# Hashed attention and a Fourier mixing block on one core: seven sorted pairs, sixteen classes, transfers in written order

## The chip, the core and the metric

The kernel runs on one core of a Trainium2 chip. The core has a matrix engine (TensorE, PE in the profile, with its weight loads as PEld), a vector engine (VectorE, DVE), a scalar engine (ScalarE, ACT), GpSimd (POOL) and SyncE (SP). SP's only work here is to issue DMA transfers; POOL issues the transfers whose rows are picked by an index (indirect DMA). The metric is the device time of one execution in microseconds (us), the median of several runs.

## What is computed

Two stages follow each other, both in float32. The first is attention in which a query sees only the keys that fall into the same hash bucket:

```
q, k, v: (4, 8, 768, 64);  proj: (64, 6)
q_bits = einsum('bhsd,dk->bhsk', q, proj) > 0      # six bits per token
q_bucket = sum(q_bits * 2**arange(6))              # 0..63; k_bucket alike
mask = q_bucket[..., :, None] == k_bucket[..., None, :]
attn = softmax(where(mask, q @ k.T / 8, -1e9))
attn_out = attn @ v
```

The second takes x, the attention's output as (4, 768, 512):

```
mixed = real(fft(fft(x, axis=1), axis=2));  u = x + mixed
un = (u - mean(u)) / sqrt(var(u) + 1e-6)
out = u + relu(un @ w_ch1) @ w_ch2                 # 512 -> 2048 -> 512
```

## The kernel before

The work goes by batch b (4) and by pair of heads n (16 in all, four per batch; a pair fills the 128 partitions with two heads of 64). `attention(b)` runs the four pairs of a batch in 24 steps, six per pair, one for each chunk of 128 keys; it yields after each step. `mix(b)` is the second stage of a batch: two folds by symmetry, a Fourier transform along the channels (tile `cs`, table `ch`, L1471) and along the sequence (tiles `A` and `B`, table `sq`, L1500), and then the two products with the weights in a seven-product scheme (`h_p`, L1777, and `o`, L1652). The main loop interleaves `attention(b)` with `mix(b - 1)`; the last `mix` runs alone. Batch 0's attention stands beside the arrival of the weights, under a manual schedule in which PE, DVE, ACT and POOL keep the written order. After it a planner orders each engine's instructions by its own estimate of times, apart from edges given by hand: `issue_after` and `behind` queue an instruction after a given one on its engine.

An **ordinary** pair computes all 768 x 768 scores: `weigh` (L1201) makes scores (L1223), exponentials (L1227) and the bucket mask (L1233), sums go into `acc` (L1359), `values` multiplies with v (L1244). Six pairs, 8, 9, 10, 12, 13 and 14 (`SORT`), are **sorted**: queries and keys are brought into the order of their buckets, so that a chunk of 128 keys needs only a window of the queries. `weigh_sorted` (L1094: scores L1106, exponentials L1110, mask L1118, sums L1125 and L1126) and `values_sorted` (L1131) work on windows of 224 or 320 columns (`SLACK` = 96 on each side). Sorting a pair has these parts:

- `rank(n)` (L880) loads q and k (L583), transposes them (L890), takes their squares for a norm (L763), computes the bits (`ubits`, L894, L900) and the bucket number of each token (`ids`, `bid`). Then, for the keys and again for the queries, it compares the numbers with 0 to 63 (`one`, L938), adds up over the six chunks (L946), counts with a matmul (`cnt`, L951), makes first and last places with a scan (L956, L959), adds it all up in PSUM (`rk`, L965 to L971), and picks each token's row (L986, L990, L996). The rows of the keys are ready some steps before those of the queries. A gap check (L977, L980) writes to `strange`: if any entry of it is positive, a flag (L1924) makes a general kernel, `_any_scores`, run after this one.
- Copies of k and v (`kvn`, and the slot of pair 3 in the last batch's x) and of q (`qnat`) are loaded on SP (L919, L927). Twelve indirect transfers on POOL scatter k and v to DRAM (`kvd`), twelve scatter q (`qsd`, all L1002).
- `fetch_sorted` (L1020) reads them back on SP in sorted order (L1023), at the first step of the pair before; `prepare_sorted` (L1051) transposes them (L1058) at the second.
- After the pair, `unsort` (L1155) transposes the result (L1159), writes it to DRAM (`osd`, L1164), gathers the rows back with twelve indirect transfers (L1172), and turns them with PE (`back`, L1182).

`ranks` (L1288) is called in every step from batch 1 on; it advances the running ranks by one part each, and starts one when its step comes (`START`, L1286): pairs 8, 9 and 10 at steps 0, 8 and 15 of batch 1, pair 12 at step 22 of it, 13 and 14 at steps 8 and 15 of batch 2.

The table `ch` is no constant tile: `mix` loads it into a part of `tq` (L1449 to L1452), whose other use is to hold temporaries of the product `o` (L1671 to L1706). The left factors of `h_p` are fetched from DRAM into a ring of 12 (w<-ad, L1745), the right factors of `o` in sets of seven (w<-bd, L1657), all on SP. `rs` (L1536, on POOL) is the row scale that the additions after `o` need.

Of the kernel before, what the change touches and what calls it, by code (L numbers as in the profile page):

```python
# [11 lines left out]
F32 = mybir.dt.float32  # L12
# [38 lines left out]
SLACK = 96  # L51


def _consts():
# [54 lines left out]
    so = np.zeros((P, 3 * P + D + 8))  # L109
# [3 lines left out]
    so[:, 3 * P : 3 * P + D] = np.arange(D)  # L113
    for r in range(P):
        h, bit = divmod(r % 32, NBITS)
        if h < 2:
            so[r, 3 * P + D + r // 32 * 2 + h] = 2.0**bit
# [382 lines left out]
def _main(  # L500
# [54 lines left out]
    SORT = (8, 9, 10, 12, 13, 14)  # L555

    def load(n, names="qkv", second=nc.sync):
# [6 lines left out]
        for nm in names:  # L564
# [14 lines left out]
            for i in range(4):  # L579
                s = src[b, 2 * t + i // 2, :, i % 2 * 32 : i % 2 * 32 + 32]  # L580
                d = tl[32 * i : 32 * i + 32]
                if nm == "k" or n in SORT:
                    nc.sync.dma_start(  # L583
                        d.rearrange("p (j a) -> p j a", a=32),
                        s.rearrange("(j b) a -> b j a", b=32),
                    )
                else:
                    s = s.rearrange("(j b r) a -> r b j a", b=32, r=2)
                    d = d.rearrange("p (r j a) -> r p j a", r=2, a=32)
                    for r in range(2):  # L590
                        nc.sync.dma_start(d[r], s[r])
# [34 lines left out]
    for i in range(NPK):  # L626
        pk = const.tile([P, 2, 2, HALF + 1], F32, tag=f"pk{i}", name=f"pk{i}")
        nc.gpsimd.memset(pk[:, :, :, HALF : HALF + 1], EPS)
        pks.append(pk)
    mean = const.tile([P, P], F32, tag="mean", name="mean")  # L630
# [241 lines left out]
    win = []  # L872
    for c in range(NT):
        win.append((max(0, c * P - SLACK), min(S, (c + 1) * P + SLACK)))
# [3 lines left out]
    eye, iota, pw8 = mb[:, 0:P].bitcast(F16), mb[:, P : P + D], mb[:, P + D : P + D + 8]  # L878

    def rank(n):  # L880

        b, t = divmod(n, NPAIR)
        load(n, "qk")
        yield
        r1 = wt([P, 3 * HALF], F32, "rank", f"rank{n}", 1)
        ut = r1[:, 0:S]
        bits = pt([P, HALF], f"ubits{n}")
        for io, nm in enumerate("qk"):
            tn = nat.pop((nm, n))
            nc.vector.transpose(ut, tn)  # L890
            norm(n, io, tn)
            for g in range(2):
                j = 2 * io + g
                nc.tensor.matmul(  # L894
                    bits[32 * j : 32 * j + 32, :], pj, ut[:, g * HALF : (g + 1) * HALF],
                    start=True, stop=True,
                )
            yield
        bt = wt([P, HALF], BF16, "bt", f"ubt{n}", 1)
        nc.vector.tensor_scalar(bt, bits, 0.0, None, op0=ALU.is_gt)  # L900
        ps = pt([P, 3, 8], f"ids{n}")
        for i in range(3):
            nc.tensor.matmul(
                ps[:, i, :], bt[:, i * P : (i + 1) * P], pw8, start=True, stop=True
            )
        bid = wt([P, 2, NT, 2], BF16, "bid", f"bid{n}")
        for io in range(2):
# [4 lines left out]
        kvn = [  # L912
            wt([P, 3, 2, 2, D], F32, "kvn", f"kvn{n}", 1),
            xs[b - 1][:, NPAIR - 1].rearrange("p (c h i d) -> p c h i d", c=3, h=2, i=2),
        ]
        for g in range(2):
            for i, src in enumerate((k, v)):
                for h in range(2):
                    nc.sync.dma_start(  # L919
                        kvn[g][:, :, h, i, :],  # L920
# [3 lines left out]
                    )  # L924
        qn = wt([P, NT, 2, D], F32, "qnat", f"qnat{n}", 1)
        for h in range(2):
            nc.sync.dma_start(  # L927
                qn[:, :, h, :], q[b, 2 * t + h].rearrange("(c p) d -> p c d", p=P)
            )
        yield  # L930
        one = r1[:, 0:HALF].bitcast(BF16).rearrange("p (c x) -> p c x", c=NT)
        upto = r1[:, HALF : 2 * HALF].bitcast(BF16).rearrange("p (c x) -> p c x", c=NT)
        kept = upto.bitcast(F16)
        m = r1[:, 2 * HALF : 3 * HALF]
        small = m.bitcast(BF16)
        total, ends = small[:, 0:P], m.bitcast(F16)
        for io in (1, 0):
            nc.vector.tensor_tensor(  # L938
                one.rearrange("p c (h x) -> p (c h) x", h=2),
                bid[:, io].rearrange("p c h -> p (c h)")[:, :, None].broadcast_to(  # L940
                    [P, 2 * NT, D]
                ),
                iota[:, None, :].broadcast_to([P, 2 * NT, D]), op=ALU.is_equal,
            )
            for c in range(2, NT + 1):
                nc.vector.tensor_tensor(  # L946
                    upto[:, c] if c < NT else total,
                    one[:, 0] if c == 2 else upto[:, c - 1], one[:, c - 1], op=ALU.add,
                )
            cnt = pt([P, P], f"cnt{io}_{n}")  # L950
            nc.tensor.matmul(cnt, onesb, total, start=True, stop=True)  # L951
            if io:
                last_, first_ = kept[:, 1], kept[:, 0]
            else:
                last_, first_ = ends[:, P : 2 * P], ends[:, 2 * P : 3 * P]
            nc.vector.tensor_tensor_scan(  # L956
                last_, onesb, cnt, 0.0, op0=ALU.mult, op1=ALU.add
            )
            nc.vector.tensor_tensor(first_, last_, cnt, op=ALU.subtract)  # L959
            yield  # L960
            ps = ps_sc.tile([P, 2, 512], F32, tag="sc", name=f"rk{io}_{n}")
            for g in range(2):
                o = ps[:, g, 0:HALF].rearrange("p (c x) -> p c x", c=3)
                cs = slice(3 * g, 3 * g + 3)
                nc.tensor.matmul(o, tri, one[:, cs], start=True, stop=False)  # L965
                if g == 0:
                    nc.tensor.matmul(o[:, 1], onesb, one[:, 0], start=False, stop=False)
                    nc.tensor.matmul(o[:, 2], onesb, upto[:, 2], start=False, stop=False)
                else:
                    nc.tensor.matmul(o, onesb, upto[:, cs], start=False, stop=False)  # L970
                nc.tensor.matmul(  # L971
                    o, eye, first_[:, None, :].broadcast_to([P, 3, P]), start=False, stop=True
                )
            if io == 0:
                gap = ends[:, 3 * P : 5 * P].rearrange("p (i x) -> p i x", i=2)
                for i, (e, f) in enumerate(((kept[:, 1], first_), (last_, kept[:, 0]))):
                    nc.vector.scalar_tensor_tensor(  # L977
                        gap[:, i], e, -float(SLACK + 1), f, op0=ALU.add, op1=ALU.subtract
                    )
                nc.vector.tensor_reduce(  # L980
                    strange[:, NW + n : NW + n + 1], gap, axis=AX.XY, op=ALU.max
                )
            rk = wt([P, NT, 2], F32, "rk", f"rk{io}_{n}", 1)
            for g in range(2):
                cs = slice(3 * g, 3 * g + 3)
                nc.vector.tensor_tensor(  # L986
                    m.rearrange("p (c x) -> p c x", c=3), one[:, cs],
                    ps[:, g, 0:HALF].rearrange("p (c x) -> p c x", c=3), op=ALU.mult,
                )
                nc.vector.tensor_reduce(  # L990
                    rk[:, cs].rearrange("p c h -> p (c h)"),
                    m.rearrange("p (c x) -> p c x", x=D), axis=AX.X, op=ALU.add,
                )
            tag, bufs = ("rowk", 1) if io else ("rowq", 7)
            rows[io, n] = wt([P, NT, 2], I32, tag, f"row{io}_{n}", bufs)
            nc.vector.tensor_copy(rows[io, n], rk)  # L996
            yield
        qsd[n] = tc.dram_tile([2 * S, D], F32, name=f"qsd{n}")
        kvd[n] = tc.dram_tile([2 * S, 2 * D], F32, name=f"kvd{n}")

        def move(io, to, c, h, src):
            ins = nc.gpsimd.indirect_dma_start(  # L1002
                to[:, :], bass.IndirectOffsetOnAxis(rows[io, n][:, c, h : h + 1], 0), src, None
            )
            group = f"rows{io}_{n}"
            tc.declare_no_dep(ins.ins, group=group, reason="rows of a permutation")
            tc.add_to_no_dep_group(group, ins.ins)
            moves.setdefault((io, n), []).append(ins.ins.name)

        for g in (1, 0):  # L1010
            for c in range(3):
                for h in range(2):
                    move(1, kvd[n], 3 * g + c, h,
                         kvn[g][:, c, h].rearrange("p i d -> p (i d)"))
        for c in range(NT):
            for h in range(2):
                move(0, qsd[n], c, h, qn[:, c, h, :])
        yield

    def fetch_sorted(n):  # L1020

        def take(io, dst, src):
            ins = nc.sync.dma_start(dst, src)  # L1023
            for name in moves[io, n]:
# [8 lines left out]
        for io, nm in enumerate("qk"):  # L1033
            tl = wt([P, S], F32, "qkn", f"{nm}s{n}", 2)
            nat[nm, n] = tl
            for i in range(4):
                h, d0 = i // 2, i % 2 * 32
                src = (kvd if io else qsd)[n][h * S : (h + 1) * S, d0 : d0 + 32]
                take(
                    io, tl[32 * i : 32 * i + 32].rearrange("p (j a) -> p j a", a=32),  # L1040
# [4 lines left out]
        for h in range(2):  # L1045
            take(
                1, tl.rearrange("p (c h d) -> p c h d", c=NT, h=2)[:, :, h, :],
# [934 lines left out]
```

## Time and profile before

| What | us |
|---|---|
| median of three runs (lowest, highest) | 1214.45 (1208.76, 1215.59) |
| the profiled execution, and its span | 1209.85, 1208.0 |
| batch 0's last pair ends | 117.7 |
| batch 1's, 2's and 3's last pair ends | 399.7, 743.4, 993.2 |
| PE, DVE, ACT, POOL busy | 1047.7, 791.1, 491.1, 292.8 |

The ends of the pairs are the starts of the copies of `vs` (L1254), one per pair. The span reaches from the first to the last instruction of the profiled execution; 1.85 us of its time lie around it. In the rows of the profile L12 is line 12 of the kernel; an arrow points from what is read to what is written; "busy" is the time in which at least one instruction of a group ran, so that overlapping matmuls count once. In a row of groups the shapes stand before the count, then busy us and mean ns of one, and behind the bar the idle time before them with what ended it.

### The profile page before, as it was taken

How to read it: one execution, taken by the hardware profiler on the slowest of the kernel's cores; microseconds unless marked ns; L12 is line 12 of the kernel's file. 1: busy time of each engine (PE TensorE's matmuls, PEld its weight loads, DVE VectorE, ACT ScalarE, POOL GpSimd, SP SyncE). 2: the span in 40 equal slices, each digit the busy share in tenths (PEclk: the TensorE clock that was granted, in tenths of full speed). 3: DMA queues.
4: the chain of work that ended last, by engine and by line, in shares of the span. 5: the costliest groups of instructions: out<-in, count | busy, mean ns of one | idle time of the engine just before them, and what ended most of it. 6: DMA issues, size and time to landing. Idle time of an engine off the chain costs nothing.

```text
span 1208.0 us, 15127 instructions
## 1 busy us (share of the span) xinstructions
PE 1047.7 (87%) x5017; PEld 651.8 (54%) x5017; DVE 791.1 (65%) x1534; ACT 491.1 (41%) x1082; POOL 292.8 (24%) x332
## 2 busy tenths in 40 slices
PE   6898888799999968797948869799899997899996
PEld 3333354347544656444734327675486466758676
DVE  6898889677999865645724739565464686435353
ACT  6896555551575302344204323135523531251330
POOL 0000043305405522361362345203221412010000
PEclk9999898899999988898969979899899999899999
DMA  8555366651355561444234611824214315030501
GB/s 247 143 104 116 67 169 165 192 124 40 88 168 186 126 222 38 95 115 89 60 106 100 133 62 48 244 37 95 66 42 148 89 38 186 28 96 20 186 22 38
DMA packets 268310, 130.99 MB, mean 108 GB/s; under 512 B 217792, under 2 KB 251328, under 8 KB 268224
## 3 DMA queue, kind: packets, MB, share of 16 engines
q1 hardware_dynamic: 257824, 115.37, 36.7%
q0 software_dynamic: 8832, 14.17, 3.6%
q8 instruction: 42, 0.69, 0.2%
q10 hardware_dynamic: 1568, 0.39, 0.1%
q14 instruction: 44, 0.36, 0.1%
HBM read 99.47 MB, written 30.41 MB: 108 GB/s over the span
## 4 chain that ended last, share of the span: by engine, by line
PE 49%; issue 11%; DVE 11%; POOL 5%; ACT 4%; another core or an unknown queue 4%; DMA 3%; DVEq 0%; SPq 0%; POOLq 0%; ACTq 0%
PE o L1652 18%; PE h_p L1777 17%; PE cs L1471 3%; POOL qsd L1002 3%; POOL kvd L1002 2%; DMA tq<-k_ch 2%; PE oo L1244 2%; PE A L1500 1%; DVE pk L1233 1%; PE oo L1140 1%; PE sc L1223 1%; PE B L1500 1%; PE sc L1106 1%; ACT rr L1278 1%
## 5 line engine op out<-in xcount | busy, mean ns | idle before, releaser
L1652 PE MATMUL o<-w,h 128*128 128x256 f32 x1152 | 264.4, 385 | 19.0 <-DVE w L1664 14.5
L1652 PEld LDWEIGHTS o<-w,h 128*128 128x128 f32 x1152 | 218.0, 192 | 62.0 <-DVE w L1664 15.0
L1777 PE MATMUL h_p<-x,w 128*128 128x384 f32 x448 | 169.1, 505 | 6.5 <-issue 2.2
L1777 PEld LDWEIGHTS h_p<-x,w 128*128 128x128 f32 x448 | 83.4, 194 | 73.0 <-issue 11.7
L1223 PE MATMUL sc<-qt,kt 64*128 64x384 f32 x480 | 103.6, 517 | 18.3 <-ACT pk L1227 8.5
L1777 PE MATMUL h_p<-w 128*128 128x384 f32 x288 | 109.7, 504 | 11.0 <-ACT w L1814 7.5
L1172 POOL DMA_INDIRECT x<-osd,row x72 | 75.7, 1052 | 148.9 <-DMA w<-ad 44.0
L1227 ACT ACTIVATE pk<-sc 128x768 f32<-128x768 f32 x120 | 92.8, 804 | 40.0 <-PE sc L1223 18.8
L1244 PE MATMUL oo<-pk,vn 128*64 128x385 f32 x480 | 99.7, 518 | 1.9 <-DVE w L666 1.3
L1002 POOL DMA_INDIRECT qsd<-qnat,row x72 | 79.9, 1110 | 69.8 <-DVE row L996 49.8
L1002 POOL DMA_INDIRECT kvd<-x,row x36 | 42.7, 1187 | 197.1 <-DVE row L996 187.7
L1777 PEld LDWEIGHTS h_p<-w 128*128 128x128 f32 x288 | 54.4, 194 | 51.6 <-ACT w L1814 10.3
L1233 DVE SCALAR_TENSOR_TENSOR pk<-qb,kb,pk 128x768 f32<-128x768 bf16 x60 | 59.5, 1011 | 26.0 <-ACT pk L1227 22.1
L1471 PE MATMUL cs<-tq,z 128*128 128x128 f32 (+3 forms) x192 | 41.2, 381 | 31.9 <-DMA tq<-k_ch 29.2
L1223 PEld LDWEIGHTS sc<-qt,kt 64*128 64x128 f32 x480 | 42.8, 192 | 44.6 <-issue 15.2
L1359 DVE TENSOR_TENSOR acc<-acc,pk 128x768 f32<-128x768 f32 (+1 forms) x48 | 63.7, 1347 | 2.6 <-ACT pk L1227 2.5
L1244 PEld LDWEIGHTS oo<-pk,vn 128*64 128x64 f32 x480 | 31.8, 141 | 61.1 <-issue 48.7
L1471 PEld LDWEIGHTS cs<-tq,z 128*128 128x128 f32 x192 | 35.1, 240 | 38.9 <-issue 30.6
L1682 ACT COPY tq<-o 128x256 f32<-128x256 f32 x24 | 8.9, 372 | 110.3 <-PE o L1652 91.4
L1664 DVE SCALAR_TENSOR_TENSOR w<-o,rs,w 128x256 f32<-128x256 f32 x56 | 26.8, 478 | 38.1 <-PE o L1652 36.0
L1536 POOL TENSOR_SCALAR rs<-mv 128x1 f32<-128x1 f32 x24 | 9.6, 402 | 167.9 <-DVE mv L1534 167.0
L1652 PE MATMUL o<-w 128*128 128x256 f32 x176 | 43.8, 393 | 2.2 <-DVE w L1664 1.1
(231 smaller groups left out, 1739.3 us busy)
## 6 DMA issues: line engine op xcount, KB each, us to landing
w<-ad SPq DMA_DIRECT2D x168, 128.0 KB
w<-bd SPq DMA_DIRECT2D x42, 512.0 KB
zraw<-in_moe_w_ch_dram SPq DMA_DIRECT2D x24, 512.0 KB
bd<-w SPq DMA_DIRECT2D x14, 512.0 KB
kn<-in_k_dram SPq DMA_DIRECT2D x60, 96.0 KB
fraw<-in_moe_w_ch_dram SPq DMA_DIRECT2D x8, 512.0 KB
ad<-tq SPq DMA_DIRECT2D x8, 512.0 KB
vn<-in_v_dram SPq DMA_DIRECT2D x20, 192.0 KB
```

The source lines that it names most:

```text
L1002: ins = nc.gpsimd.indirect_dma_start(to[:, :], bass.IndirectOffsetOnAxis(rows[io, n][:, c, h : h + 1], 0), src, None)
L1172: nc.gpsimd.indirect_dma_start(x[:, j * D : (j + 1) * D], None, osd[n][:, :], bass.IndirectOffsetOnAxis(rows[0, n][:, c, h : h + 1], 0),)
L1223: last[0] = nc.tensor.matmul(ps[:, h, 0:HALF], kt[rows, ks], qt[rows, qs], start=kb is not None, stop=True,)
L1227: nc.scalar.activation(pk[:, g, :, 0:HALF], ps[:, :, 0:HALF], AF.Exp, scale=SCALE)
L1233: nc.vector.scalar_tensor_tensor(w, qb[:, h].rearrange("p (g s) -> p g s", g=2), kb[:, h, c : c + 1], w, op0=ALU.is_equal, op1=ALU.mult,)
L1244: nc.tensor.matmul(oos[g][h * D : (h + 1) * D, 0:w], nat["v", n][:, (2 * c + h) * D : (2 * c + h + 1) * D], pk[:, g, h, 0:w], start=(c == ...
L1359: nc.vector.tensor_tensor(acc[:, g], (first if c == 1 else acc)[:, g], new[:, g], op=ALU.add,)
L1471: nc.tensor.matmul(ps[:, pc + 2 * lo : pc + 2 * hi - 1 : 2], z[:, cp, pc, par, t * P : (t + 1) * P], ch[:, cp, pc, lo:hi], start=(cp == 0) ...
L1500: nc.tensor.matmul(ps[:, cols], F[:, par, k, t, j * P : (j + 1) * P], sq[:, t, k, cols], start=(t == 0), stop=(t == 1),)
L1652: nc.tensor.matmul(ps, a[:, r], right7[i][:, r], start=start and r == 0, stop=r == HF // 2 - 1, skip_group_check=not start,)
L1664: nc.vector.scalar_tensor_tensor(t[:, cols], src, r, t[:, cols], op0=ALU.mult, op1=ALU.add)
L1777: nc.tensor.matmul(ps, left[:, k], right[i][:, k], start=start and k == 0, stop=k == 1, skip_group_check=not start,)
```

## The change

- Pair 6, the third of batch 1, joins the sorted pairs.
- The rank sorts by 16 classes, the upper four of the six bits, in one pass for queries and keys together. The windows are given by two lists instead of `SLACK` (together 1816 columns instead of 1728). The mask still compares all six bits. The check now tests for each chunk that no class of its keys has queries outside of the window, and that too goes to `strange`.
- `pin` keeps a transfer behind everything written before it on its queue (SP or POOL); all transfers of the sort get it. `trailing` queues the rank's matmuls and the transposes of `back` behind the last matmul of the scores.
- The scatter goes in groups of six, one group in each step: the first half of k and v, two groups of q, then the second half of k and v, which is loaded into the tile that q leaves (`kvn`, now shared; `qnat` goes). The gather in `unsort` goes in two groups of six. `kvd`, `qsd` and `osd` are split by head.
- The fetch of a sorted pair comes one step later (two for pair 6), `unsort` begins one step later.
- The ranks start at step 21 of batch 0 (pair 6), at steps 3, 9 and 15 of batch 1 (8, 9, 10) and of batch 2 (12, 13, 14); `ranks` is called in batch 0 too.
- `rk` moves from the scores' PSUM buffers to the shared ones (`pt`).
- `ch` becomes a constant tile, loaded once behind the first weights.

```diff
-SLACK = 96
+NCL = 16
+WIN_LO = (0, 32, 152, 264, 400, 536)
+WIN_HI = (216, 368, 504, 608, 736, 768)
...
-    SORT = (8, 9, 10, 12, 13, 14)
+    SORT = (6, 8, 9, 10, 12, 13, 14)
...
+    ch = const.tile([P, 2, 2, DM // 2], F32, tag="ch", name="ch")
...
+    def pin(made):
+        tc.keep_in_program_order(made)
+        return made
+    @contextmanager
+    def trailing():
+        with tc.issue_after(last[0].ins):
+            yield
...
+        nc.vector.tensor_tensor(
+            one.rearrange("p o c (h x) -> p (o c h) x", h=2),
+            bid.rearrange("p o c h -> p (o c h)")[:, :, None].broadcast_to(
+                [P, 4 * NT, NCL]
+            ),
+            iota[:, None, :].broadcast_to([P, 4 * NT, NCL]), op=ALU.is_equal,
+        )
...
+        yield
+        cnt = pt([P, 2 * W], f"cnt{n}")
+        with trailing():
+            nc.tensor.matmul(cnt, onesb, total, start=True, stop=True)
...
+        natural(kv0, 0)
+        for h in range(2):
+            pin(nc.sync.dma_start(
                 qn[:, :, h, :], q[b, 2 * t + h].rearrange("(c p) d -> p c d", p=P)
+            ))
+        yield
+        ps = pt([P, HALF], f"rk{n}")
+        o = ps.rearrange("p (o c x) -> p o c x", o=2, c=NT)
+        with trailing():
+            nc.tensor.matmul(o, tri, one, start=True, stop=False)
+            nc.tensor.matmul(
+                o[:, :, 1:NT], onesb, upto[:, :, 1:NT], start=False, stop=False,
+            )
+            nc.tensor.matmul(
+                o, eye,
+                first_.rearrange("p (o x) -> p o x", o=2)[:, :, None, :].broadcast_to(
+                    [P, 2, NT, W]
                 ),
+                start=False, stop=True,
+            )
...
+        move_kv(kv0, 0)
+        for g in range(2):
+            yield
+            for c in range(3 * g, 3 * g + 3):
+                for h in range(2):
+                    move(0, c, h, qn[:, c, h, :])
+        yield
+        kv1 = wt([P, 3, 2, 2, D], F32, "kvn", f"kvn{n}", 1)
+        natural(kv1, 1)
+        yield
+        move_kv(kv1, 1)
         yield
...
     def prepare_sorted(n):
+        yield
+        if n < 2 * NPAIR:
+            yield
         fetch_sorted(n)
...
-    START = {1: {8: 0, 9: 8, 10: 15}, 2: {12: -2, 13: 8, 14: 15}}
+    START = {1: {6: -3}, 2: {8: -21, 9: -15, 10: -9}, 3: {12: -21, 13: -15, 14: -9}}
...
-                if b:
-                    ranks(b, t, c)
+                ranks(b, t, c)
...
     def mix(b):
         x = xs[b]
-        ch = tq.rearrange("p i n -> p (i n)")[:, 0 : 2 * DM].rearrange(
-            "p (c k n) -> p c k n", c=2, k=2
-        )
-        nc.sync.dma_start(ch, cn["ch"].ap())
         yield from fold(b, 1)
...
     next(other)
+    nc.sync.dma_start(ch, cn["ch"].ap())
```

## The prediction

> **What bounds the kernel now.** I read the page's busy shares first, then the engines' busy time in five stretches cut where a batch's last pair ends (batch 0; batches 1, 2 and 3; the tail after the last pair), then the waits of PE, then the chain of waits. The page:
>
> ```profile
> PE 1047.7 (87%) x5017; PEld 651.8 (54%) x5017; DVE 791.1 (65%) x1534; ACT 491.1 (41%) x1082; POOL 292.8 (24%) x332
> ```
>
> PE is busy for 87% of the span, so what it does and what it waits for set the time. By stretch (the first numbers are the stretch, its length, PE busy; then PEld, DVE, ACT, POOL, the granted clock, DMA share and GB/s):
>
> ```profile
> 0.00:118.00 118.00, 98.69 (x664) 40.56 (x664) 98.36 (x172) 89.84 (x176) 1.46 (x17) 1.00 0.62 154
> 118.00:400.00 282.00, 252.65 (x1144) 137.08 (x1144) 241.75 (x465) 144.75 (x307) 81.76 (x72) 0.95 0.49 133
> 400.00:743.00 343.00, 273.55 (x1257) 172.29 (x1258) 199.00 (x404) 103.79 (x243) 133.36 (x143) 0.89 0.40 100
> 743.00:993.00 250.00, 228.27 (x1134) 152.45 (x1132) 153.26 (x296) 96.19 (x223) 62.06 (x73) 0.97 0.35 93
> 993.00:1208.00 215.00, 194.50 (x825) 149.43 (x821) 98.71 (x202) 56.52 (x135) 14.15 (x28) 0.96 0.26 82
> ```
>
> Batch 1 (118 to 400) is nearly full on PE (90%) and on DVE (86%): work removed there shortens it. Batch 2 (400 to 743) has 70 us in which PE does nothing. Two waits explain much of that idle time. One is the reload of the Fourier table into tq, in the waits of PE:
>
> ```profile
> PE cs L1471 <- DMA tq<-k_ch: 29.2, 3, 10.8
> ```
>
> Three times, once at the start of each mix from the second on, PE stands still for 8 to 11 us. The other shows in the chain of waits (start, length, what) as time that no engine accounts for:
>
> ```profile
> 541.62 8.71 another core or an unknown queue
> ...
> 606.35 10.29 another core or an unknown queue
> 616.66 0.18 DVE kb L866
> 616.84 8.88 another core or an unknown queue
> ```
>
> With smaller pieces these make up the page's 3.6% of the chain, 43 us. The pieces over 1 us all lie inside or just behind runs of row transfers on POOL. In its timeline the run from 592 to 623 is 24 transfers, one every 1.25 us:
>
> ```profile
> 606.89 0.94 POOL L1172 DMA_INDIRECT x<-osd,row  x1 [0.30 <-issue]
> 608.13 0.95 POOL L1172 DMA_INDIRECT x<-osd,row  x1 [0.31 <-issue]
> 609.39 0.95 POOL L1172 DMA_INDIRECT x<-osd,row  x1 [0.30 <-issue]
> ```
>
> Meanwhile DVE waits for a PE result (kb, L862) that PE's own rows show finished at 606.6. Why, the trace doesn't say.
>
> **A. The table stays resident.** The load of ch in each mix (L1452) goes; one load of 512 KB is added near the start. At 443.0, 773.8 and 1019.6 the last product is over and z has been ready for 5 to 11 us (its last copies, L1442, are at 438.0, 764.0 and 1008.1), so PE can go on at once. Next in line is the evacuation of the last products, at most 1 us each. 29.2 - 3 = 26 us. The windows behind the gaps show a second part:
>
> ```profile
> 1019.60:1030.40 10.80, 0.01 (x1) 0.04 (x1) 2.73 (x6) 0.00 (x0) 1.74 (x4) 0.61 0.76 257
> 1030.40:1035.60 5.20, 5.20 (x16) 4.53 (x17) 0.00 (x0) 0.65 (x2) 0.00 (x0) 0.50 0.01 3
> 1035.60:1041.00 5.40, 5.40 (x40) 5.19 (x39) 0.00 (x0) 4.08 (x12) 0.00 (x0) 1.00 0.00 0
> ```
>
> After the gap the granted clock is 0.50 and 16 matmuls take 5.20 us; at 1.00, 40 take 5.40. The same holds for 8.8 us behind the gap at 443 and 4.5 us behind the one at 774: 18.5 us at half clock. If half of that were saved it would be 9 us; ACT's copies of F follow closely at full clock (4.08 us busy of 5.40), so I take 7, between 0 and 9. [...] A: -33 us; from -24 (5 us of other waits come up, nothing from the clock) to -38 (29.2 + 9).
>
> **B. Cheaper ranks and one ordinary pair less.** The ranking rows that shrink, for six pairs:
>
> ```profile
> L986 DVE TENSOR_TENSOR rank<-rank,rk 128x384 f32<-128x384 bf16 x24 | 13.2, 549 | 10.7 <-remote 8.9 <-PE rk L971 1.6
> L946 DVE TENSOR_TENSOR rank<-rank 128x128 bf16<-128x128 bf16 x60 | 13.1, 219 | 1.0
> L990 DVE TENSOR_REDUCE rk<-rank 128x6 f32<-128x384 f32 x24 | 13.1, 546 | 0.3
> L938 DVE TENSOR_TENSOR rank<-bid,mean 128x768 bf16<-128x768 bf16 x12 | 11.4, 948 | 10.6 <-ACT bid L908 10.6
> ```
>
> With the scans, differences, gaps, the maximum and the casts (4.9 + 3.3 + 2.9 + 2.5 + 2.0) DVE spends 66.4 / 6 = 11.1 us per pair. Afterwards q and k go through one pass over 384 instead of two over 768: the comparison is half of 0.95, five additions and a copy of 64 elements lie between the 0.16 us of a 4-element copy (L1442) and 0.22 each, then scan, difference, four window tests and a maximum on 32 to 64 elements (0.2 to 0.3 each), one product and one sum (0.55 each) and a cast: about 4.5 us. DVE saves 6 x 6.6 = 39 us. On PE cnt and rk cost 27.9 / 6 = 4.65 us per pair; one cnt (0.23) and three rk matmuls (0.33) are 1.2: 6 x 3.4 = 21 us less.
>
> Pair 6 as an ordinary pair costs PE 103.6 / 10 for scores and 111.6 / 10 for values, 21.5 us; a sorted pair (25.8 + 38.4) / 6 = 10.7, plus ranking and putting back: 1.75 (ubits) + 1.2 + 0.5 (ids) + 0.95 (back) = 4.4. PE: -6.4. On DVE masks and sums fall from 11.9 + 8.7 to 5.8 + 2.7; two transposes, the bits, the rank and the transpose back add 8.0: -4. The windows grow from 1728 to 1816 columns, 5% of 10.7 us in seven pairs: +3.8 us on PE.
>
> So PE loses some 17 us in batch 1, 9 in batch 2, and gains 2 in batch 3. Worth the share in which PE is busy there (0.9, 0.8): 15 + 7 - 2 = 20 us. Bounds: 0, if DVE or a transfer sets the pace, and 24, if all of it counts.
>
> **C. What is added ahead.** Pair 6's rank begins in the last pair of batch 0, where every engine keeps the written order and DVE is busy 24.1 of 26 us: two transposes and the bits are 2.5 us more. Their eight loads are issued only after pair 4's norm, 0.52 us each on SP, and DVE transposes q one step (4.3 us) later: it may wait for data up to 5 us, with the mask work behind it, and PE behind that. The table's load takes 512 KB of a queue that moves 218 GB/s there: up to 2.4 us. I take +5, from 0 to 10.
>
> **D. Order and grouping of the sort's transfers.** Each is now queued behind all that is written before it on SP or POOL. On SP a wait for a buffer (kvn, which q and the second half of k and v share) now holds up the w<-ad fetches written after it; these run up to 12 products ahead, about 24 us of PE (each is 4 matmuls of 0.5 us), against some 16 us of q moves (12 x 1.3), so that costs nothing unless two such waits meet. Behind POOL's transfers stand rs (needed half a stage later), stores that nobody waits for, and F's memset. All sorts start at or near their old steps and keep 6 steps or more before their fetch, except pair 6, with one. The fetch comes one step later, with one step (10 to 16 us) left before its transposes; ten issues are 5 us. So the order alone is worth nothing either way. The grouping may act on the 43 us of unexplained waits. The trace has no run split into sixes. From below: they vanish, -43. From above: each of seven pairs gets a stall like that of 606 to 626, 7 x 19 = 133, +90. The nearest rows: the two runs of 24 hold 19.2 (592 to 623) and 8.5 us (705 to 715), the others some 15 together; runs of 24 arise where moves of one pair meet the return of another, which the later, separate steps make rarer. I take half of their 27.7, -14, and give back 4 for 36 more transfers: -10.
>
> **Sum.** -33 - 20 + 5 - 10 = -58 us. The profiled execution took 1209.85 us (span 1208.0): 1152. The median of the three runs shown is 4.6 us above it, so 1156 is predicted for the median.
>
> **Rivals.**
> - Waits vanish altogether: D is -43, and the rest stands. 1156 - 33 = 1123, to 1108 with A and B at their ends. For it: every large piece lies at a run of transfers. Against: q's and k's ranks now come together, so 18 transfers can leave in one run if nothing else is queued between.
> - The gain is hidden: PE's saved work turns into waits for transposes or fetches, as L1068 (DVE for PE bits, 18.1 us) and the fetches of L1023 already show; only A's waits are left and D is 0: 1214 - 26 + 5 = 1193, or 1178 with a part of B. For it: batch 2 has 70 us of PE idle, which less PE work does not remove.
> - Slower: the unexplained waits grow with the runs of 18. The price is up to 19 us per sorted pair in batches 1 and 2, 133 in all, 90 more than now; it outweighs the 48 us of A to C once a pair loses over 13 us ((43 + 48) / 7) on average. 1220 to 1256.
> - It doesn't do what it says: a class of the inputs reaches out of its window, the flag at L1924 is set and the general kernel runs after the fast one. That would about double the time. The inputs are fixed; I give it 1%.
>
> **How the numbers follow.** The forecast (1140 to 1178) has 0.50, waits gone 0.20, gain hidden 0.18, slower 0.08, same 0.03, the flag 0.01. A measurement here tells about 0.5% (6 us) from no change. Faster by more than that: 0.50 + 0.20 + 0.18 = 0.88, less 0.01 for the upper end of the hidden case: 0.87; within: 0.04; slower: 0.09. The range runs from 1108 to 1200: it takes in the first three cases, 0.88 of the chance, less their tails.
>
> **What would show it.** A: no wait of cs for k_ch, and a clock of 1.0 where each mix begins. B: batch 1 some 15 us shorter, the DVE rank rows near 4.5 us per pair, batch 2 at least 15 shorter. C: PE idle in the last pair of batch 0, DVE waiting for qn. D: the share of "another core or an unknown queue" in the chain, and how long POOL's runs are. I am wrong if PE waits for w<-ad or w<-bd, or if that share grows.

## The result and the profile after

The changed kernel takes **1285.03 us** (median of 4 runs, 1273.70 to 1287.76) against 1214.05 of the kernel before: a ratio of 1.0575, with a 95% interval of 1.0504 to 1.0646. It is slower by 71 us where 58 less were forecast. The profiled execution took 1285.94 us, 1284.1 of them its span; 1.84 lie around it, as before. So the loss is inside the span: 76 us between the two profiles. One execution of run e15 below, the profiled one, took 1523 us at a mean granted clock of 0.65, where its others took 1156 to 1160, and is left out.

The page after, the busy shares first:

```profile
PE 1066.6 (83%) x4947; PEld 651.9 (51%) x4947; DVE 754.1 (59%) x1483; ACT 490.2 (38%) x1087; POOL 323.5 (25%) x368
```

DVE has 37 us less to do, as part B wanted, and PE's share fell from 87 to 83%: no engine became the bound, they all wait more. The stretches, cut at the new ends of the batches, with the columns of the table of before:

```profile
0.00:125.00 125.00, 99.66 (x646) 40.73 (x648) 99.84 (x173) 90.62 (x176) 1.45 (x17) 0.96 0.61 152
125.00:458.00 333.00, 270.74 (x1166) 149.10 (x1162) 225.70 (x460) 142.09 (x312) 123.92 (x115) 0.92 0.43 117
458.00:814.00 356.00, 264.83 (x1160) 157.30 (x1158) 168.32 (x341) 103.22 (x238) 119.81 (x132) 0.86 0.38 95
814.00:1081.00 267.00, 239.50 (x1162) 157.29 (x1161) 159.70 (x301) 97.86 (x226) 64.72 (x77) 0.97 0.34 91
1081.00:1284.00 203.00, 191.89 (x823) 147.43 (x820) 100.58 (x211) 56.38 (x135) 13.63 (x28) 0.99 0.27 85
```

Batch 0 is 7 us longer, batch 1 51, batch 2 13, batch 3 17; only the tail is 12 shorter. Batch 1, where pair 6 is sorted now, lost most, though DVE has 16 us less to do in it. In batch 2 PE is idle for 91 us.

The chain of waits says of what kind the loss is. "Another core or an unknown queue" had 44 us of it before (the prediction rounds it to 43); now it has 107, with this piece the longest (start, length, what):

```profile
581.13 0.96 DVE qb L564
582.09 0.47 DVE h L1852
582.55 34.43 another core or an unknown queue
```

I call it the **unaccounted time**. The timeline inside that piece:

```profile
584.40 0.23 PE L1198 MATMUL oo<-pk,vs 128*64 128x1 f32 x4
...
600.17 0.97 POOL L1040 DMA_INDIRECT qsd<-qn,rows  x1 [0.30 <-issue]
600.88 0.16 ACT L1307 COPY vs<-oo 128x1 f32<-128x1 f32 x1 [14.84 <-remote]
```

ACT's copy needs only the product `oo` that PE's rows show finished at 584.6, and stands idle for 14.84 us until 600.9. Meanwhile POOL issues row transfers, one every 1.25 to 1.28 us, 30 in a row from 574 to 612. The longest wait of PE (waited for, us in total, times, longest) lies in the same run:

```profile
PE kb L1134 <- issue: 23.8, 1, 23.8
```

The six transfers of a step do not stay six: POOL keeps the written order, waits for a load or a store of results, and then fires all that has queued up (it waits 104.5 us in all for loads of k and v, and 73.2 for stores of results). Before, nearly all runs had 12 transfers or fewer, and two had 24; now they have 18 (three times), 24 (twice) and 30 (twice), apart from the sixes and three twelves.

### The profile page after: what moved, and what is told of

Read it like the earlier page. It is cut to its first block, busy times and chain, and to the rows that moved or that the text cites. A ratio compares the mean times of both kernels' runs of the same rounds, so it can differ in the third digit from the quotient of the medians.

```text
span 1284.1 us, 14975 instructions
## 1 busy us (share of the span) xinstructions
PE 1066.6 (83%) x4947; PEld 651.9 (51%) x4947; DVE 754.1 (59%) x1483; ACT 490.2 (38%) x1087; POOL 323.5 (25%) x368
## 4 chain that ended last, share of the span: by engine, by line
PE 53%; DVE 12%; another core or an unknown queue 8%; ACT 7%; issue 4%; DMA 3%; SPq 1%; POOL 1%; DVEq 0%; ACTq 0%; POOLq 0%
PE o L1701 20%; PE h_p L1826 18%; PE oo L1297 2%; PE sc L1156 2%; PE oo L1190 2%; PE A L1549 1%; PE B L1549 1%; DMA zraw<-in_moe_w_ch_dram 1%; PE sc L1276 1%; ACT rr L1331 1%; PE cs L1520 1%; DVE acc L1413 1%; DVE pk L1286 1%; ACT pk L1280 1%
## 5 line engine op out<-in xcount | busy, mean ns | idle before, releaser
L1224 POOL DMA_INDIRECT x<-osd,rows x84 | 91.1, 1084 | 188.0 <-DMA osd<-ot 73.2
L1297 PE MATMUL oo<-pk,vn 128*64 128x384 f32 (+1 forms) x432 | 100.5, 533 | 10.7 <-ACT x L1310 9.0
L1276 PE MATMUL sc<-qt,kt 64*128 64x384 f32 x432 | 93.5, 526 | 13.6 <-ACT pk L1280 11.1
L1280 ACT ACTIVATE pk<-sc 128x768 f32<-128x768 f32 x108 | 83.4, 806 | 47.5 <-remote 22.1
L1040 POOL DMA_INDIRECT qsd<-qn,rows x84 | 89.5, 1065 | 25.6 <-issue 25.6
L1286 DVE SCALAR_TENSOR_TENSOR pk<-qb,kb,pk 128x768 f32<-128x768 bf16 x48 | 47.0, 1011 | 54.4 <-ACT pk L1280 50.9
L1040 POOL DMA_INDIRECT kvd<-kvn,rows x42 | 46.7, 1111 | 115.6 <-DMA kvn<-in_v_dram 104.5
L1040 POOL DMA_INDIRECT kvd<-x,rows x42 | 43.1, 1026 | 97.8 <-DVE rows L1033 85.9
L1413 DVE TENSOR_TENSOR acc<-acc,pk 128x768 f32<-128x768 f32 (+1 forms) x44 | 56.7, 1310 | 12.3 <-ACT pk L1280 12.1
L1168 DVE SCALAR_TENSOR_TENSOR pk<-qb,kb,pk 128x336 f32<-128x336 bf16 (+4 forms) x84 | 40.7, 526 | 13.3 <-ACT pk L1160 9.2
```

The costliest lines, as they stand in the source:

```text
L1040: ins = pin(nc.gpsimd.indirect_dma_start((kvd if io else qsd)[n, h][:, :], bass.IndirectOffsetOnAxis(rows[n][:, io, c, h : h + 1], 0), src ...
L1168: nc.vector.scalar_tensor_tensor(w, qb[:, h, lo:hi], kb[:, h, c : c + 1], w, op0=ALU.is_equal, op1=ALU.mult,)
L1224: pin(nc.gpsimd.indirect_dma_start(x[:, j * D : (j + 1) * D], None, osd[n, h][:, :], bass.IndirectOffsetOnAxis(rows[n][:, 0, c, h : h + 1] ...
L1276: last[0] = nc.tensor.matmul(ps[:, h, 0:HALF], kt[rows, ks], qt[rows, qs], start=kb is not None, stop=True,)
L1280: nc.scalar.activation(pk[:, g, :, 0:HALF], ps[:, :, 0:HALF], AF.Exp, scale=SCALE)
L1286: nc.vector.scalar_tensor_tensor(w, qb[:, h].rearrange("p (g s) -> p g s", g=2), kb[:, h, c : c + 1], w, op0=ALU.is_equal, op1=ALU.mult,)
```

## The experiments

**Theories.** 1: the order kept on SP and POOL costs, since a transfer that waits holds up what is queued behind it. 2: the unaccounted time costs, and it comes with longer runs of row transfers. Beside these: pair 6 is not worth its work.

The runs fell on several chips, and that matters. A is the chip of the result (its number is not on record, so it may be C or E); e1 to e8 ran on B, e9 to e12 on C, e13 to e16 on D, e17 and e18 on E. The kernel before was run beside them on each, so only the ratios are compared between chips. In the table, the last column is the unaccounted time in the chain of the run's profile, its pieces added up (before on A: 44).

| run | the changed kernel, but | chip | us | before, us | ratio (95% interval) | unaccounted, us |
|---|---|---|---|---|---|---|
| result | - | A | 1285.0 | 1214.1 | 1.0575 (1.0504, 1.0646) | 107 |
| e1 | groups of six paced by the steps | B | 1167.0 | 1134.3 | 1.0257 (1.0204, 1.0311) | 0 |
| e2 | no order kept | B | 1127.8 | 1134.3 | 0.9934 (0.9912, 0.9955) | 0 |
| e3 | six pairs | B | 1132.9 | 1134.3 | 0.9987 (0.9953, 1.0020) | 0 |
| e4 | ch reloaded | B | 1180.6 | 1134.3 | 1.0380 (1.0330, 1.0430) | 0 |
| e5 | nothing | B | 1158.8 | 1133.5 | 1.0214 (1.0156, 1.0273) | 0 |
| e6 | (the kernel before) | B | 1132.6 | 1133.5 | | 0 |
| e7 | order kept on SP only | B | 1189.8 | 1133.5 | 1.0511 (1.0467, 1.0555) | 0 |
| e8 | order kept on POOL only | B | 1106.0 | 1133.5 | 0.9756 (0.9728, 0.9785) | 0 |
| e9 | e8, six pairs | C | 1172.6 | 1209.2 | 0.9718 (0.9666, 0.9770) | 50 |
| e10 | e8, ch reloaded | C | 1238.8 | 1209.2 | 1.0236 (1.0175, 1.0298) | 109 |
| e11 | e8, and SP's order for the fetches | C | 1252.6 | 1209.2 | 1.0365 (1.0307, 1.0422) | 83 |
| e12 | e8, and SP's order for the loads | C | 1220.5 | 1209.2 | 1.0104 (1.0073, 1.0135) | 100 |
| e13 | as e8 | D | 1105.7 | 1134.9 | 0.9749 (0.9713, 0.9784) | 0 |
| e14 | as e9 | D | 1105.8 | 1134.9 | 0.9767 (0.9724, 0.9810) | 0 |
| e15 | as e11 | D | 1157.9 | 1134.9 | 1.0205 (1.0168, 1.0242) | not read |
| e16 | e9, scatters of k, v twice | D | 1153.3 | 1134.9 | 1.0174 (1.0136, 1.0211) | 0 |
| e17 | e8, second half of k, v from POOL | E | 1227.0 | 1212.4 | 1.0137 (1.0073, 1.0201) | 81 |
| e18 | e17, six pairs | E | 1180.6 | 1212.4 | 0.9731 (0.9703, 0.9760) | 72 |

### Pace, order, pair 6, table

e1, ahead of each group of six POOL now copies an element that DVE took from the step's `pk`:

```diff
+        mk = wt([1, 2], F32, "mk", f"mk{paced[0]}", 8)
+        nc.vector.tensor_copy(mk[:, 0:1], pks[(npk[0] - 1) % NPK][0:1, 0, 0, 0:1])
+        pin(nc.gpsimd.tensor_copy(mk[:, 1:2], mk[:, 0:1]))
```

> The changed kernel, but ahead of each group of six row transfers POOL copies one element that DVE took from the weights of the step the group belongs to; so a group can't start before its step, and runs of 18 to 30 transfers break up. Theory 'runs' (the waits that no engine accounts for, 43 us of the chain before and about 107 after, come from long runs of back-to-back row transfers on POOL): the runs fall to 6 or 12, those waits to under 45 us, the time from 1285 to 1200-1235 us. Rival 'order' (queueing behind everything written holds back fetches and loads): the pins are all still there, so the time stays within 1270-1310 us. Rival 'pair 6' (the seventh sort itself, in batch 1): also no change, 1270-1310 us.

e2:

```diff
     def pin(made):
-        tc.keep_in_program_order(made)
         return made
```

> The changed kernel without the edges that keep the sort's transfers behind what is written before them; the planner places them on SP and POOL as it did before. Theory 'runs': the time follows the length of POOL's runs, whatever it comes out at; with runs like those of the changed kernel (30) it stays above 1260 us, with runs of 12 it falls below 1220. Rival 'order': it falls by most of the 71 us, to 1200-1230 us, whatever the runs are. Rival 'pair 6': 1270-1300 us.

e3:

```diff
-    SORT = (6, 8, 9, 10, 12, 13, 14)
+    SORT = (8, 9, 10, 12, 13, 14)
-    START = {1: {6: -3}, 2: {8: -21, ...
+    START = {2: {8: -21, ...
```

> The changed kernel with pair 6 ordinary again (six sorted pairs, nothing of the sort in batch 0). Theory 'runs': batch 1 loses its waits and gets back some 10 us; batches 2 and 3 keep the runs of 24 to 30 and their waits, so 1245-1275 us. Rival 'pair 6': batch 0 and batch 1 together get back the 58 us that they lost, 1215-1235 us. Rival 'order': 1250-1280 us.

e4, in `mix` (the constant tile and its load go):

```diff
+        ch = tq.rearrange("p i n -> p (i n)")[:, 0 : 2 * DM].rearrange(
+            "p (c k n) -> p c k n", c=2, k=2
+        )
+        nc.sync.dma_start(ch, cn["ch"].ap())
```

> The changed kernel with the table of the channel transform loaded into tq at each mix again, as before. If the resident table is worth what the prediction took for it, 24 to 38 us come on top: 1309-1323 us, with three or so waits of PE for that load of about 10 us each. If another wait takes the place of the removed one, the time stays within 1280-1295 us.

Measured: 1.0257, 0.9934, 0.9987 and 1.0380, and none of the four profiles has any unaccounted time, so the theory of the runs could not be tested on B. What separates them is something else: against e5 below, which has no edit, the kept order costs 2.8% (e2) and, with that order kept, pair 6 2.3% (e3) where no time is missing. Pacing shows no effect there (its interval overlaps that of e5), and it broke the runs of transfers only in part: half of e1's runs are sixes, but four of 24 to 30 are left.

### The changed kernel again, and the order queue by queue

e5 and e6 have no edit.

> The changed kernel as it is, beside the kernel before. In the runs so far the pair of kernels stood at 1.0575, with 107 us of the changed kernel's chain in no engine's account. Four variants of it that ran on another chip had no such time at all, and there the kernel before takes 1134 us. Theory 1 (the cost lies in the order that the change imposes on SP and POOL, and the unaccounted time only adds to it): the ratio lies between 1.02 and 1.04, near that of the variant that also reloads the table (1.038) or paces the transfers (1.026), whether the unaccounted time shows or not. Theory 2 (the cost is the unaccounted time, which longer runs of row transfers cause): where that time is missing from the profile the ratio is 0.95 to 0.99.

> The kernel before as it is, for its profile on the chip of this call. If this is a chip without the unaccounted time, the share of another core or an unknown queue is 0 in its chain too, its end of batch 2 comes some 40 to 60 us earlier than in the first profile (743), and the waits of PE for the table k_ch are still 25 to 30 us. If the time is there, the share is 3 to 4%.

e5 gives 1.0214, so theory 1's range holds and theory 2's does not: on a chip without unaccounted time the change still loses. The chains' shares by engine, of e5 and then of e6, show that the time is absent for both kernels:

```profile
PE 53%; DVE 13%; POOL 7%; ACT 6%; issue 5%; DMA 4%; SPq 1%; DVEq 0%; POOLq 0%; ACTq 0%
```

```profile
PE 53%; DVE 20%; issue 4%; ACT 4%; DMA 3%; POOL 3%; SPq 0%; DVEq 0%; ACTq 0%; POOLq 0%
```

In e6 batch 2 ends at 675.5, 68 us earlier than on A, and the waits for k_ch are the same 29.2 us. e7 drops the order on POOL, e8 that on SP:

```diff
-            ins = pin(nc.gpsimd.indirect_dma_start(
+            ins = nc.gpsimd.indirect_dma_start(      # e7; the gathers of unsort too
...
-            ins = pin(nc.sync.dma_start(dst, src))
+            ins = nc.sync.dma_start(dst, src)        # e8; all loads and stores of the sort too
```

> The changed kernel with the written order kept for the sort's transfers on SP only; POOL's row transfers stand where the planner puts them. Theory 1a (SP's order costs: fetches of right and left factors stand behind transfers that wait for a tile): no better than the changed kernel, within 0.8% of it. Theory 1b (POOL's order costs: stores and row scales stand behind row transfers that wait): nearly all of the gain of the kernel without any kept order, 0.99 to 1.00 of the kernel before. Theory 2 (long runs of row transfers): between, with the runs shorter than 18 to 30.

> The changed kernel with the written order kept on POOL only; SP's transfers of the sort stand where the planner puts them. Theory 1a (SP's order costs): nearly all of the gain of the kernel without any kept order, 0.99 to 1.00 of the kernel before. Theory 1b (POOL's order costs): no better than the changed kernel, within 0.8% of it. If both orders must be gone together, both this and the last are slow.

It is SP's order that costs (1a): e8 is 4.6% faster than e5 and beats the kernel before. POOL's order is worth having, which 1a did not foresee: without it (e7) the kernel is 3% slower than e5, and with neither order (e2) 1.8% slower than e8. In e7 PE waits for rows that come back late:

```profile
PE back L1235 <- DMA x<-osd,rows: 16.7, 13, 7.4
```

How SP's order costs is in its timeline (the start of the first, time to the end of the last of a group; SP's rows count the issue, not the wait). e5, around the fetch of a pair in batch 3:

```profile
725.60 10.68 SPq L1706 DMA_DIRECT2D w<-bd  x7
736.58 0.91 SPq L999 DMA_DIRECT2D kvn<-in_k_dram  x2
737.53 1.02 SPq L999 DMA_DIRECT2D kvn<-in_v_dram  x2
738.71 0.49 SPq L1510 DMA_DIRECT2D F<-k_sq  x1
739.24 6.51 SPq L1070 DMA_DIRECT2D qs<-qsd  x4
```

Seven right factors of the product `o` (w<-bd, a set that waits until the products of the set before are done) come first, and the fetch of the sorted rows, written after them, follows at 739. DVE then stands idle for 9.06 us until its transpose at 748, PE for 6.4. SP's wait for that set from 700 to 745 (in us: total, times, longest), and all waits of PE in e5 for transposes of fetched rows:

```profile
SPq L1706 <- PE o L1701: 44.4, 7, 36.5
```

```profile
PE bits L1112 <- DVE qt L1108: 11.8, 3, 6.4
PE bits L1112 <- DVE kt L1108: 6.3, 3, 3.2
```

Neither wait of PE is in e8's list. They are 18 of the 36 us by which PE is idle longer in e5 than in e8; the rest is spread over small waits. PE is also busy 19 us longer (1038.0 against 1018.8) at a lower mean granted clock (0.965 against 0.979). In e8 the planner put half of the same fetch ahead of that set:

```profile
689.93 4.76 SPq L1794 DMA_DIRECT2D w<-ad  x8
694.80 0.94 SPq L1070 DMA_DIRECT2D qs<-qsd  x2
695.84 9.16 SPq L1706 DMA_DIRECT2D w<-bd  x7
```

### Which part of SP's order, and what pair 6 is worth

e9 is e8 with the edit of e3, e10 is e8 with that of e4. e11 and e12 are e8 with a part of SP's order put back:

```diff
+            ins = pin(nc.sync.dma_start(dst, src))            # e11: fetch_sorted, L1070
...
+                        pin(made)                             # e12: load, L598
+                    pin(nc.sync.dma_start(to[:, :, h, i, :],  # e12: natural, L999
+            pin(nc.sync.dma_start(qn[:, :, h, :],             # e12: L1009
```

> The changed kernel with the written order kept on POOL only, and with six sorted pairs as before (pair 6 is an ordinary one again). If the loss has two independent parts, the order on SP in batches 2 and 3 and pair 6 in batches 0 and 1, this has neither. Summed from stages: batches 0 and 1 as with six pairs and all pins (117 and 279 us), batches 2 and 3 and the tail as with POOL's order only (248, 233, 202): 1079 us of span, a ratio to the kernel before of 0.95. If what pair 6 costs in batch 1 is work that comes back as a gain in batch 2, no better than 0.975.

> The changed kernel with the written order kept on POOL only, and with the table loaded into tq in every mix again. Part A of the prediction, the resident table, was put at 33 us: then this takes 1132 to 1140 us, a ratio of 1.00 (0.976 plus 0.029). If the wait for the table only covers other waits, the difference to the kernel with POOL's order only is under 12 us.

> The changed kernel with the written order kept on POOL, and on SP for the fetches of sorted rows only (L1070). Theory X (the fetches stand behind refills of the right and left factors that wait up to 36 us for a product, and come too late for the transposes): most of the loss of the full order is back, a ratio of 1.00 to 1.02. Theory Y (the loads of k, v and q, which wait for their tile, hold up the factor fetches written after them): this is as fast as with POOL's order only, 0.97 to 0.98.

> The changed kernel with the written order kept on POOL, and on SP for the loads of q, k and v (L598, L999, L1009) only, not for the fetches of sorted rows nor the stores of results. Theory X (late fetches): 0.97 to 0.985. Theory Y (loads that wait for their tile hold up the factors): 1.00 to 1.02. If the loads are themselves late behind the factors, and so the scatter and the fetch, also 1.00 or more, but then PE waits for transposes of sorted rows and not for factors.

These four ran on chip C, where every profile has unaccounted time: 50 us with six pairs (the texts below put it at 41), 83 to 109 with seven. The base e8 was not measured there, so they are only compared with each other: the fetches' order costs 2.6% more than the loads' order (e11 against e12), and PE's waits for transposes of fetched rows are there with it (10.6 us in e11) and absent without it (e10, e12). The sum of stages for e9, 0.95, was not reached: 0.972. On D the base ran beside them:

> The changed kernel with the written order kept on POOL only, once more, beside its variants. On a chip like the second one (kernel before 1134 us, no unaccounted time) 0.976 again. On a chip like the last one (kernel before 1209, unaccounted time in every profile): 1.00 to 1.01, since with six pairs it is 0.972 there and pair 6 cost 2.3% on the other chip, and as pair 6 brings row transfers, its unaccounted time should be 70 to 100 us against 41 us with six pairs.

> POOL's order only and six sorted pairs, once more. On a chip without unaccounted time the sum of stages gives 1079 us of span, a ratio of 0.95; on one with it, 0.972 again with some 40 us unaccounted.

> POOL's order, and SP's order for the fetches of sorted rows only, seven pairs. Theory X (the fetches come late behind waiting refills): 2.5 to 4.5% over POOL's order alone in this call, and PE waits for the transposes of sorted rows (bits) in batches 2 and 3. Theory Y (it is the loads): within 1% of POOL's order alone.

e15 against e13 on D: 1157.9 - 1105.7 = **52 us for the order of the fetches on SP alone**, as much as the whole of SP's order on B (e5 against e8: 53). Theory X holds; at 4.7% the cost is a little above its range. e14 against e13: with six pairs it is as fast as with seven (0.9767 and 0.9749, within their intervals), so **pair 6 is worth nothing** there. My sum of stages (0.95) was wrong because stages share work: with six pairs batch 0 is 11 us shorter than in e13, batch 1 3, but batch 2 is 14 longer.

Where the rest of the expected gain went, the profile of e14 shows. PE stops twice for 11 us (from 319.5 and 609.5). SP's timeline ahead of the first:

```profile
319.36 0.92 SPq L999 DMA_DIRECT2D kvn<-in_k_dram  x2
...
323.60 0.41 SPq L725 DMA_DIRECT2D zraw<-in_moe_w_ch_dram  x1
```

From 300 to 319 SP issues nothing: the second half of k waits for its tile `kvn`, which the change lets q share, until POOL's last rows of q have left it (the chain: the transfer of 317.14, then L999). A weight fetch stands behind it, and DVE, in order, behind that:

```profile
328.31 0.43 DVE L671 TENSOR_SCALAR w<-zraw 128x512 int32<-128x512 int32 x1 [13.15 <-DMA zraw<-in_moe_w_ch_dram]
```

The mask that PE waits for is DVE's next instruction but one (L1286). The stop at 609 is of the same kind, with SP empty from before 585 to 604 and a fetch of sorted rows behind the load, for which DVE waits 14.2 us. In all, SP waits at that load for

```profile
SPq L999 <- DMA qsd<-qn,rows: 104.6, 13, 38.2
```

e16 is e9 with each scatter of k and v issued a second time, into a tile that nobody reads:

```diff
+            if io:
+                ins = pin(nc.gpsimd.indirect_dma_start(
+                    kve[n, h][:, :],
+                    bass.IndirectOffsetOnAxis(rows[n][:, 1, c, h : h + 1], 0), src, None,
+                ))
```

> POOL's order only and six sorted pairs, and every scatter of k and v is issued a second time into a spare tile that nobody reads: 72 row transfers more, 90 us more on POOL. Theory P (on the chips that show it, the unaccounted time comes with the runs of row transfers on POOL): unaccounted time grows from 41 us by 15 to 35 us and the kernel gets as much slower. Theory Q (the unaccounted time has another source and only falls there): it stays at 35 to 45 us and the kernel within 1%. On a chip without unaccounted time both expect within 1% of six pairs, since POOL is busy a quarter of the span.

Chip D has no unaccounted time, so P and Q are not told apart. But both expected less than 1% there, and it costs 4.2% (47 us): a miss that speaks for the hold-up just shown. POOL has room (busy for 32% of the span), the tiles have not; SP's waits in e16, where e14 has 104.6 and 23.8 us:

```profile
SPq L999 <- DMA qsd<-qn,rows: 131.9, 18, 37.4
...
SPq L1009 <- DMA kve<-kvn,rows: 73.8, 8, 19.0
```

### The loads off SP

```diff
-        natural(kv1, 1)
+        natural(kv1, 1, nc.gpsimd)      # from POOL's queue
```

> POOL's order only, seven pairs, and the second half of k and v (tile kvn, which it must wait for until q's rows have left it) is loaded from POOL's queue instead of SP's. Theory Z (what is left of the loss is SP held at these loads, with fetches of factors and weights queued behind them: 82 us of SP waiting in the profile, of which 14 pieces up to 32 us): the kernel gains 5 to 15 us over POOL's order alone, a ratio of 0.962 to 0.970 on a chip like the second. Against it: within 0.5% of 0.975, SP's wait has cover.

> The same with six sorted pairs. With SP's order gone its profile still had two stops of PE of 11 us, both behind SP waiting for kvn with a weight or a factor queued behind. Theory Z: both go, 15 to 25 us, a ratio of 0.955 to 0.963 on a chip like the second (0.95 to 0.96 on the slow one, where six pairs took 0.972). If pair 6 has any worth of its own, the kernel with seven pairs is now the faster of the two; if not, this one.

These ran on E, a chip with unaccounted time (81 and 72 us), and the base was not beside them, so theory Z stays open: SP's wait for q's rows is gone from the list of e17, but 0.9731 for e18 misses the 0.95 to 0.96 expected for such a chip and is not better than the 0.9718 of e9 on C. What the two do show is pair 6 on such a chip: 1227.0 - 1180.6 = 46 us, where on D it cost nothing.

**A version that beats the kernel before** on both chips where it ran: order kept on POOL only and six pairs, 0.9718 on C, 0.9767 on D. On B and D seven pairs do as well (0.9756, 0.9749). The changed kernel itself did not run on C and D.

## Why the prediction was wrong, step by step

**D is the step that failed**, twice, and so the sign.

- "The order alone is worth nothing either way." I asked what stands behind the sort's transfers on SP, and found cover. I did not ask what the sort's transfers now stand behind. The prediction gave a fetch one step, 10 to 16 us, and five for its ten issues; a set of w<-bd ahead of it waited up to 36.5 us (e5). Measured: 52 us on D (e15 against e13), shown by putting back that one order. Nor is POOL's order worth nothing: it gains some 20 us on B (e8 against e2).
- Grouping: -10 was taken between -43 and +90. In the profiles on A the unaccounted time rose from 44 to 107 us, **+63**; that the grouping is its cause was not shown. The rival for it was on record ("the unexplained waits grow with the runs of 18", decided at 13 us per pair) with a chance of 0.08; it is 107 / 7 = 15.3 us per pair. The argument "the later, separate steps make them rarer" was wrong: the steps separate the writing, but POOL, held in order, empties in runs of 18 to 30. Its range ended at 1256 because the fetches' 52 us were not in it.

Without D the direction was right, the size not. Where no time is unaccounted for, the change minus SP's order gains 29 us (e13, on D), and with no order kept at all 6.5 (e2, on B), where A, B and C came to -48.

- **A, -33**: the wait of cs for k_ch is gone, the granted clock is 1.0 where the last three mixes begin (0.5 before), and the tail is 12 us shorter on A, 12 in e5 against e6. The clock's part was 7; PE's rows for cs, of before and of after, give 6.5:

```profile
L1471 PE MATMUL cs<-tq,z 128*128 128x128 f32 (+3 forms) x192 | 41.2, 381 | 31.9 <-DMA tq<-k_ch 29.2 <-ACT F L1484 2.2 <-DVE bt L1068 0.5
```

```profile
L1520 PE MATMUL cs<-ch,z 128*128 128x128 f32 (+3 forms) x192 | 34.7, 338 | 5.7 <-ACT F L1527 3.8 <-DVE rank L1027 1.4 <-ACT F L1533 0.5
```

  In all, taking it back costs 1.7% on B (e4 1.0380, e5 1.0214), 19 us, and 10 to 28 by their intervals; on C e10 is 18 us slower than e12, which keeps the table and a part of SP's order. The mechanism is right, the size near its lower bound of 24 or below; what fills the rest of the gap was not tried.
- **B, -20**: the operations shrank as said: the rank's rows on DVE from comparison to cast add up to 31.4 us for seven pairs, 4.5 each. PE's rows for rk and cnt fell from 27.5 us (e6, six pairs) to 8.1 (e13, seven; a fall of 21 was forecast for six). But batch 1 is not 15 us shorter; it is 16 longer in e5 than in e6, and 51 on A, and batch 2, forecast at least 15 shorter, is 4 shorter in e5 and 13 longer on A. One term that failed is pair 6: PE is busy 1017.7 us with seven pairs (e13) and 1013.9 with six (e14), so instead of -6.4 it is +4, with its stall in batch 0 on top. Even without it batch 1 does not shrink (278.6 us in e3, 278.1 in e6), so the cheaper ranks show no gain there either; where their saving went was not traced.
- **C, +5**: 7 on A, 8 on B (e5 against e6; e3, without pair 6, none). The size is right, the wait only in part. PE does stand at the bits for 10.4 us until DVE has transposed q, whose loads were issued at 103.6:

```profile
116.46 0.98 DVE L921 STREAM_TRANSPOSE rank<-qn 128x768 f32<-128x768 f32 x1
```

```profile
117.58 1.50 PE L926 MATMUL ubits<-rank,pj 128*32 128x384 f32 x4 [10.38 <-DVE rank L921]
```

  But DVE never waits for that data, as the prediction had it: it works without a pause from 103.7 on and comes to the transpose, in written order, at 116.5.
- "I am wrong if PE waits for w<-ad or w<-bd, or if that share grows": the share grew, from 3.6 to 8.4%. No wait of PE for a factor is in its list; the fetch of rows waited behind them.

Put together with measured terms for A, as an estimate: -29 + 52 + 63 = +86 against 76 in the two spans. The terms come from different chips, and late releases and late fetches can lie over each other.

**Open.** Why an engine is released so long after the result that it needs is done, on some chips and not on others; whether the runs of transfers cause it (the kernel with doubled scatters, e16, ran on D, where there is none); and why pair 6 costs 46 us on E when the chains of e17 and e18 differ by only 10 us of unaccounted time. Shorter runs were tried on B only (e1), where there is no unaccounted time to lose.

## What to carry to other kernels

When a transfer is pinned to its written place, look at both sides of it: what it will hold up, and how long the instruction ahead of it in that queue can wait (in e5 the set of w<-bd ahead of a fetch waited up to 36.5 us, and DVE then stood idle for 9.06 us until the fetched rows were there). Put the order only on the queue that needs it (here POOL's, worth 2 to 3%), and leave a queue that carries refills to the planner. Be careful with two transfers of one queue that share a tile when the second must wait for another engine to empty it: in e14 SP stood 104.6 us at such loads (that taking them off SP helps was not shown).

## What the runs showed of the hardware

Chips differ, for one and the same kernel: the kernel before takes 1214, 1209 and 1212 us on A, C and E, and 1134 and 1135 on B and D, 6 to 7% less. On A, C and E every profile has unaccounted time (44 to 109 us), and 94 to 99% of it (96% in both profiles on A) lies inside POOL's runs of row transfers or within 2 us of their ends, though these take only 24 to 28% of the span (216 or 252 transfers, one every 1.28 or 1.27 us by the median on A, before and after); on B and D there is none, with long runs at the same pace there too (in e3 on B 23 transfers in a row, one every 1.28 us by the median, in e16 on D 29 in 39 us, one every 1.27). On A a run of 12 has at most 9 us of it, runs of 24 and 30 up to 32. That it coincides is shown; that the runs cause it is not. In one such run on A, of 30 transfers, ACT waited 14.84 us for a product of PE that was done; what held it was not shown.
